# Windowed attention and gated MLP on one core: pairs 0 and 1 loaded and set up ahead of a branch, masks, weights and sinks moved in time, the end spread over four engines

## The chip, the cores and the metric

The kernel runs on one core of one Trainium2 chip. The metric is device time in microseconds of one execution of the whole program, constants, weight conversion, attention and MLP together; lower is better. The core's engines named here are TensorE (PE in the rows, its weight loads PEld), VectorE (DVE), ScalarE (ACT), GpSimd (POOL) and SyncE (SP), which issues nearly all DMAs.

## The reference

Causal attention with a window and a few sink positions, then an MLP whose hidden layer goes through a depthwise convolution of three taps and gates itself:

```python
# q, k, v: (4, 8, 768, 64); n_sink = 4, window = 128 (both are inputs)
rel  = pos[:, None] - pos[None, :]
keep = (pos[None, :] < n_sink) | ((rel >= 0) & (rel < window))
s = np.where(keep, q @ k.T / sqrt(64), -1e9)
a = softmax(s)                                 # sum + 1e-9
x = (a @ v) -> (4, 768, 512)                   # heads side by side
h = maximum(x @ w_in, 0)                       # (4, 768, 1024)
conv = sum over k of conv_w[k] * h shifted by k - 1 along seq
out = (h * sigmoid(conv)) @ w_out              # (4, 768, 512)
```

The activations are float32; w_in, w_out and conv_w reach the kernel as 64-bit floats.

## The kernel before

**Precision.** Each matrix product of two float32 values is made as three products of halves (high x high, low x high, high x low) in TensorE's single-pass 32-bit type. So nearly every tensor passes a split: one engine copies it to the narrow type (xH, gH, wH), another subtracts to get the remainder (xL, gL, wL). Weights come as 64-bit floats; `narrow` puts the two words of each together, with one multiply on ScalarE (L112) and shifts and ors on VectorE, and `split` makes the halves on GpSimd and VectorE.

**Branch.** n_sink and window are loaded into `sc`, copied over all partitions. VectorE makes a flag of them (window between 1 and 128, at most four sinks), every engine reads it, and the program branches to `banded` (which runs here) or to `general`. Up to the branch the first halves of q and k of pair 0 and a half of v are loaded, and an identity matrix is made.

**Attention.** Heads are taken in pairs, 16 pairs, four to a batch. Batch 0 goes in half sequences, all four pairs' first halves and then the second ones; later batches go pair by pair. A job is cut in steps of one row tile of 128. q and k of a half are turned by TensorE (tiles `trq`, `trk`, L319) and copied out and scaled by ScalarE (L250), kinds `X`/`bq` and `kks`/`kk`; then scores on TensorE, mask and row minimum on VectorE (L541, L542), exp on ScalarE (L545), sums and reciprocals on VectorE, scaling on GpSimd. One step later the probabilities are turned (`pT`, L568), and two or three steps later multiplied with v (`pv`). A sink is one of the first four positions; where it lies outside the tile's window its values come from `vsr`, a small tile that holds the v rows of the sinks in split form. It is filled for batch 0 by `sink_load` (L385) and for each later batch by `sink_split` (three loads L396, a copy on ScalarE L397, VectorE L398 to L400, copies by DMA L405). Output of a tile is `px`, split into xH (ScalarE, L351) and xL (VectorE, L352).

**MLP.** `unit` makes one block of 128 hidden rows over 256 positions: 12 matmuls into `ph` (L184: wH·xH, wL·xH, wH·xL, four each), ReLU on ScalarE, the convolution and the gate on ScalarE and VectorE in turn (L191 to L199), the split of the result g (GpSimd, L201 and L202), and 6 matmuls into `po` (L211) which collect over the hidden blocks; after the last block `po` is copied out by ScalarE (L215) and stored (L216). These units are the work that fills TensorE between the steps of the next batch's attention; the last batch's units come after all attention.

**Order.** The code is written in one loop over the steps (D1 = 1, D2 = 2, DL = 3 steps back), with MLP pieces, weights (one per step, list WHEN) and the next job's preparation between the slots. A scheduler then reorders it by simulated times and priorities: steps of attention have a high priority. So code order alone does not say where an instruction stands in its engine's queue. Each engine's queue runs in order. Tiles of the tag "h" are three buffers of TensorE's output memory that q, k, `ph` and other turns share; `pts` is one buffer for turned probabilities of batch 0.

**Masks.** The masks m0, w1 and w2 and the primitives they are made from (`before`, `sk`, `inw`, `prv`, from iotas R and C) stand at the start of `banded`, all on VectorE but for the copy w2 <- w1 (L444, ScalarE) and two narrow copies (L449). GpSimd's memsets there clear `A.zeros` (L454) and `c.vs` (L457); `vsr` is cleared by two DMAs from `A.zeros` (L460).

Of the kernel before, what the change touches and what calls it, by code (L numbers as in the profile page):

```python
# [17 lines left out]
P = 128  # L18
# [43 lines left out]
class Moe:  # L62
# [41 lines left out]
    def narrow(self, raw):  # L104
# [5 lines left out]
        w, low = (self.temp("st", 512, 3)[0:rows, 0:n] for i in range(2))  # L110
        lo, hi, wi, li = raw[:, :, 0], raw[:, :, 1], w.bitcast(I32), low.bitcast(I32)
        nc.scalar.mul(low, f(hi), 2.0 ** -112)  # L112
# [12 lines left out]
    def taps(self, raw):  # L125
        c, nc = self.c, self.c.nc
        w = self.narrow(raw)
        pt = self.ps.tile([P, 512], F32, tag="h", name="cwt", bufs=3)
        c.pin(nc.tensor.transpose(pt[:, 0:3 * self.NFF], w, c.ident[0:3 * self.NFF, 0:3 * self.NFF]))
        nc.scalar.copy(self.cw.rearrange("p k f -> p (k f)"), pt[:, 0:3 * self.NFF])  # L130

    def weights(self):
# [14 lines left out]
        self.raws = []  # L147
        self.done = 0
# [6 lines left out]
    def need(self, n):  # L155

        while self.done < n:
            self.fetch(self.done + 1)
            self.todo[self.done][2](self.raws[self.done])
            self.done += 1  # L160
            self.fetch(self.done + LA)

    def unit(self, n):
# [12 lines left out]
        u = Ctx()  # L176

        def first(lo):
            if lo == 0:
                self.need(max(self.place[f"wi{ff * P // 512}_{self.NCC - 1}"], self.place["taps"]) + 1)  # L180
                u.h = self.ps.tile([P, 512], F32, tag="h", name=f"ph{n}", bufs=3)
            for i in range(lo, lo + 4):
                w, x, cc = prods[i]
                c.pin(nc.tensor.matmul(u.h[:, 0:W], w[:, cc, ff * P:(ff + 1) * P], x[:, cc, t0:t1],  # L184
                                       start=(i == 0), stop=(i == len(prods) - 1)))
# [3 lines left out]
        def gate():  # L189
# [46 lines left out]
class Attn:  # L236
# [20 lines left out]
    def prep(self, g, s, ahead=lambda: None):  # L257
# [20 lines left out]
        def turn_k(half):  # L278
# [24 lines left out]
            if half == 0 and kw > P:  # L303
# [84 lines left out]
def sink_split(c, m, vsr, b):  # L388
# [4 lines left out]
    both = m.mp.tile([P, 512, 2], F32R, tag="nat", name=f"sink{b}", bufs=3).rearrange("p n w -> p (n w)")[0:3 * NS]  # L393
    lo, hi = both[:, 0:512], both[:, 512:1024]
    for part in range(3):
        nc.sync.dma_start(f(lo[NS * part:NS * part + NS]).rearrange("s (h d) -> s h d", d=D), c.v[b].rearrange("h s d -> s h d")[0:NS])  # L396
    nc.scalar.copy(hi, f(lo))  # L397
# [10 lines left out]
def banded(c):  # L408
# [17 lines left out]
    before = cp.tile([P, P], F32, name="before")  # L426
    wprev = cp.tile([P, 1], F32, name="wprev")
    tmps = [m.temp("st", 512, 3) for i in range(2)]
    R, C, inw, sk, tmp, prv = [tmps[i // 3][:, P * (i % 3):P * (i % 3) + P] for i in range(6)]
    c.iotas(R, C)  # L430
    nc.vector.tensor_scalar(before, R, 0.0, None, ALU.is_lt)
    nc.vector.tensor_scalar(sk, C, c.nsv, None, ALU.is_lt)
    nc.vector.tensor_scalar(tmp, R, 0.0, None, ALU.is_ge)
    nc.vector.scalar_tensor_tensor(out=inw, in0=R, scalar=c.wnv, in1=tmp, op0=ALU.is_lt, op1=ALU.mult)
    nc.vector.tensor_scalar(wprev, c.wnv, -float(P), None, ALU.add)
    nc.vector.tensor_scalar(prv, R, wprev, None, ALU.is_lt)
# [7 lines left out]
    nc.scalar.copy(w2, w1)  # L444
    nc.vector.tensor_scalar(w2[:, P:KW], sk[:, 0:NS], -NEG, NEG, ALU.mult, ALU.add)

    def narrow_masks():
        for mk, w in ((m1, w1), (m2, w2)):
            nc.scalar.copy(mk[:, 0:NS], w[:, P:KW])  # L449
# [16 lines left out]
    c.headscale = cp.tile([P, 2], F32, name="headscale")  # L466
    nc.gpsimd.memset(c.headscale, 0.0)
    for j in range(2):
        nc.gpsimd.memset(c.headscale[D * j:D * j + D, j:j + 1], -1.0 / math.sqrt(D))
# [19 lines left out]
    for i, (g, nm, half) in enumerate(queue[0:2]):  # L489
        st[g].raw[nm, half] = c.raw[i]  # L490
    asked = [2]

    free = [RAWB - 2]
# [22 lines left out]
    def scores(g, t):  # L516
# [369 lines left out]
```

## Time and profile before

| | us |
|---|---|
| time, median of 3 runs | 480.58 (479.12 to 481.94) |
| the profiled execution's own time | 479.95 |
| its span on the chip | 478.2 |
| TensorE busy | 447.2 (94%) |
| VectorE busy | 335.9 (70%) |
| ScalarE busy | 321.9 (67%) |
| GpSimd busy | 281.1 (59%) |
| mean granted clock of TensorE (1 is full) | 0.996 |

The span runs from the first to the last instruction of the profiled execution; 1.75 us of its time lie outside. All rows below have their times in us from the start of the span. A row names an engine, a line of the kernel, an operation, and the tiles as out<-in.

### The profile page before, as it was taken

How to read it: one execution, taken by the hardware profiler on the slowest of the kernel's cores; microseconds unless marked ns; L12 is line 12 of the kernel's file. 1: busy time of each engine (PE TensorE's matmuls, PEld its weight loads, DVE VectorE, ACT ScalarE, POOL GpSimd, SP SyncE). 2: the span in 40 equal slices, each digit the busy share in tenths (PEclk: the TensorE clock that was granted, in tenths of full speed). 3: DMA queues.
4: the chain of work that ended last, by engine and by line, in shares of the span. 5: the costliest groups of instructions: out<-in, count | busy, mean ns of one | idle time of the engine just before them, and what ended most of it. 6: DMA issues, size and time to landing. Idle time of an engine off the chain costs nothing.

```text
span 478.2 us, 10559 instructions
## 1 busy us (share of the span) xinstructions
PE 447.2 (94%) x3181; PEld 389.6 (81%) x3181; DVE 335.9 (70%) x1186; ACT 321.9 (67%) x1026; POOL 281.1 (59%) x561
## 2 busy tenths in 40 slices
PE   1888978998999999999999999999999999999993
PEld 1666767897888988898989898988989898988982
DVE  4789989757868668696775858587866653665561
ACT  3898767759868868776775867676866744554541
POOL 3465667633956658667665657567666752445441
PEclk9999999998999999999999999999999999999999
DMA  5778873377695664827273564626361101000001
GB/s 145 202 208 224 238 226 70 77 179 164 162 210 134 160 144 92 206 67 167 69 184 94 122 156 100 157 65 154 75 162 26 45 1 45 0 19 27 31 16 52
DMA packets 105707, 55.91 MB, mean 117 GB/s; under 512 B 83056, under 2 KB 98440, under 8 KB 105640
## 3 DMA queue, kind: packets, MB, share of 16 engines
q1 hardware_dynamic: 105640, 55.13, 46.5%
q8 instruction: 28, 0.46, 0.4%
q14 instruction: 39, 0.32, 0.2%
HBM read 28.17 MB, written 6.29 MB: 72 GB/s over the span
## 4 chain that ended last, share of the span: by engine, by line
PE 68%; DVE 13%; POOL 4%; DMA 4%; ACT 4%; issue 2%; SPq 1%; DVEq 0%; ACTq 0%; POOLq 0%
PE ph L184 24%; PE po L211 23%; PE px L618 7%; PE pts L580 3%; PE sc L344 3%; PE sc L343 3%; PE px L641 2%; PE tq L267 2%; DVE stm L115 1%; DVE t L196 1%; DVE stm L114 1%; DVE t L197 1%; PE tk L293 1%; POOL pe L550 1%; DMA wi_1r<-in_moe_w_in_dram 1%
## 5 line engine op out<-in xcount | busy, mean ns | idle before, releaser
L211 PE MATMUL po<-woH,g 128*128 128x512 f32 x384 | 138.0, 405 | 3.4 <-POOL g L201 3.1
L184 PE MATMUL ph<-xH,wiH 128*128 128x258 f32 (+1 forms) x384 | 111.5, 291 | 2.1 <-DVE xL L352 2.1
L184 PE MATMUL ph<-xH,wiL 128*128 128x258 f32 (+1 forms) x384 | 109.5, 285 | 0.0
L184 PE MATMUL ph<-xL,wiH 128*128 128x258 f32 (+1 forms) x384 | 109.4, 286 | 0.0
L201 POOL TENSOR_SCALAR g<-t 128x256 fp32r<-128x256 f32 x96 | 44.5, 464 | 75.1 <-DVE t L199 56.7
L550 POOL TENSOR_SCALAR pe<-pe,sm 128x132 f32<-128x132 f32 (+1 forms) x144 | 64.1, 457 | 41.7 <-DVE sm L548 27.2
L211 PEld LDWEIGHTS po<-woH,g 128*128 128x128 f32 x384 | 69.4, 189 | 15.3 <-POOL g L201 5.5
L196 DVE SCALAR_TENSOR_TENSOR t<-hb,cw,t 128x256 f32<-128x256 f32 x96 | 53.6, 559 | 37.5 <-ACT t L195 37.1
L202 POOL TENSOR_TENSOR g<-t,g 128x256 fp32r<-128x256 f32 x96 | 74.8, 780 | 5.7
L184 PEld LDWEIGHTS ph<-xH,wiH 128*128 128x128 f32 x384 | 72.8, 190 | 4.9 <-issue 2.5
L211 PE MATMUL po<-woL,g 128*128 128x512 f32 x192 | 76.1, 397 | 0.0
L184 PEld LDWEIGHTS ph<-xH,wiL 128*128 128x128 f32 x384 | 72.9, 190 | 2.2
L184 PEld LDWEIGHTS ph<-xL,wiH 128*128 128x128 f32 x384 | 72.8, 190 | 1.2
L545 ACT ACTIVATE pe<-pe,sm 128x132 f32<-128x132 f32 (+1 forms) x144 | 57.9, 403 | 19.0 <-DVE sm L542 18.1
L198 ACT ACTIVATE t<-t 128x256 f32<-128x256 f32 x96 | 39.9, 417 | 35.2 <-DVE t L197 34.7
L199 DVE SCALAR_TENSOR_TENSOR t<-t,hb 128x256 f32<-128x256 f32 x96 | 46.1, 480 | 16.6 <-ACT t L198 15.4
L195 ACT ACTIVATE t<-hb,cw 128x256 f32<-128x256 f32 x96 | 48.8, 510 | 12.1 <-POOL g L202 9.3
L197 DVE SCALAR_TENSOR_TENSOR t<-hb,cw,t 128x256 f32<-128x256 f32 x96 | 52.0, 541 | 3.9
L191 ACT ACTIVATE hb<-ph 128x258 f32<-128x258 f32 (+1 forms) x96 | 36.8, 384 | 18.9 <-PE ph L184 13.1
L541 DVE COPY_PREDICATED sc<-before,sc 128x128 f32<-128x128 int32 x120 | 32.9, 288 | 18.4 <-PE sc L344 17.8
L618 PE MATMUL px<-pT,vraw 128*64 128x128 f32 (+1 forms) x512 | 42.6, 316 | 2.0 <-ACT pT L568 1.7
L542 DVE CUSTOM_DVE_ANT_0 pe<-sc,m 128x132 f32<-128x132 f32 (+1 forms) x144 | 39.4, 285 | 5.0 <-PE sc L344 4.6
(150 smaller groups left out, 906.9 us busy)
## 6 DMA issues: line engine op xcount, KB each, us to landing
X<-bq SPq DMA_DIRECT2D x96, 96.0 KB
vraw<-in_v_dram SPq DMA_DIRECT2D x16, 384.0 KB
out_dram<-stm SPq DMA_DIRECT2D x24, 256.0 KB
kk<-kk SPq DMA_DIRECT2D x24, 198.0 KB
raw<-in_k_dram SPq DMA_DIRECT2D x24, 192.0 KB
raw<-in_q_dram SPq DMA_DIRECT2D x24, 192.0 KB
kk<-bk SPq DMA_DIRECT2D x48, 96.0 KB
raw<-in_q_dram SPq DMA_DIRECT2D x16, 96.0 KB
```

Source lines behind the costliest of these rows:

```text
L184: c.pin(nc.tensor.matmul(u.h[:, 0:W], w[:, cc, ff * P:(ff + 1) * P], x[:, cc, t0:t1], start=(i == 0), stop=(i == len(prods) - 1)))
L195: nc.scalar.mul(a, prev, cw[:, 0, ff:ff + 1])
L196: nc.vector.scalar_tensor_tensor(out=e, in0=this, scalar=cw[:, 1, ff:ff + 1], in1=a, op0=ALU.mult, op1=ALU.add)
L197: nc.vector.scalar_tensor_tensor(out=a, in0=nxt, scalar=cw[:, 2, ff:ff + 1], in1=e, op0=ALU.mult, op1=ALU.add)
L198: nc.scalar.activation(e, a, AF.Tanh)
L199: nc.vector.scalar_tensor_tensor(out=a, in0=e, scalar=1.0, in1=this, op0=ALU.add, op1=ALU.mult)
L201: nc.gpsimd.tensor_scalar(u.g[:, 0], a, 1.0, 1.0, ALU.mult, ALU.mult)
L202: nc.gpsimd.tensor_tensor(out=u.g[:, 1], in0=a, in1=f(u.g[:, 0]), op=ALU.subtract)
L211: c.pin(nc.tensor.matmul(po[:, 0:c.DM], u.g[:, a, tt * P:(tt + 1) * P], w[:, ff, :], start=(ff == 0 and i == 0), stop=(ff == NFF - 1 and i ...
L545: nc.scalar.activation(pe[:, j, cols], pe[:, j, cols], AF.Exp, bias=sm[:, j:j + 1], scale=-1.0, accum_out=sm[:, 2 + 2 * j:3 + 2 * j])
L550: nc.gpsimd.tensor_scalar(pe[:, j, cols], pe[:, j, cols], sm[:, 8 + j:9 + j], 1.0, ALU.mult, ALU.mult)
L618: ins = nc.tensor.matmul(px[h][D * j:D * j + D, P * at:P * at + n], s.v[:, j, kt, :], pT, start=(h not in open_), stop=False, skip_group_c ...
```

## The change

1. **Loads.** The first halves of q and k of pairs 0 and 1 are loaded ahead of the branch (four slots in place of two); the first half of v goes behind it.
2. **Set-up.** `headscale`, the iotas and the primitives of the masks are made ahead of the branch; three of them carry a dependency (`follow`) on the operation that makes the flag. `follow(c, a, b)` makes a wait for b. The primitives lie in the second v buffer.
3. **Masks.** The copy w2 <- w1 goes to VectorE; GpSimd's two memsets wait for the last mask operation; the two narrow copies wait for the last turned tile; the clearing of `vsr` moves to the middle of batch 0.
4. **Weights.** The first multiply of each `narrow` waits for the exp two steps back (`c.exps[-2]`). The taps are written to another tile and are turned later.
5. **Turns.** In the first halves, every second turn of probabilities uses an "h" tile in place of `pts`; the copy of k's sink columns of the first half moves to the second half's turn.
6. **Sinks.** `sink_split` is cut in two: the loads are issued at the first step of a batch (`sink_fetch`), the split three steps later for every batch (before: at once for batch 1), behind that step's last exp.
7. **End.** The last two units are split on ScalarE and VectorE in place of GpSimd; the unit that has two units behind it (TRAIL) starts its second products only behind the newest first product; the last block of the output is copied by VectorE and ScalarE, half each, and stored by SP's and ScalarE's queues.

The order of ScalarE's queue right behind the branch, before (`trq` and `trk` are the turned q and k, `kks` and `X` their copies, `roomH` rows hold probabilities and masks, `wi_0r` is the first weight):

```order
L250 ACTIVATE kks_155<-trk_187 128x3x128
L328 COPY kks_155<-kks_155 128x6x4
L444 COPY roomH<-roomH 128x260
L449 COPY m_132<-roomH 128x4
L112 ACTIVATE stm_260<-wi_0r 128x512
L449 COPY m_133<-roomH 128x4
L250 ACTIVATE X_184<-trq_180,headscale 128x384 x2
L250 ACTIVATE X_228<-trq_224,headscale 128x384 x2
L545 ACTIVATE roomH,sm_161<-roomH,sm_161 128x128 x2
```

The same place after the change:

```order
L288 ACTIVATE X_182<-trq_178,headscale 128x384 x2
L288 ACTIVATE kks_159<-trk_185 128x3x128
L366 COPY kks_159<-kks_159 128x6x4
L288 ACTIVATE X_224<-trq_220,headscale 128x384 x2
L580 ACTIVATE roomH,sm_163<-roomH,sm_163 128x128
L288 ACTIVATE kks_159<-trk_243 128x3x128
L580 ACTIVATE roomH,sm_163<-roomH,sm_163 128x128
L366 COPY kks_159<-kks_159 128x6x4
L118 ACTIVATE stm_256<-wi_0r 128x512
```

The two copies of q and the first exp have moved ahead of the first weight, and the mask copies are gone.

SP's queue right behind the branch, before:

```order
L101 DMA wi_0r<-in_moe_w_in_dram 128x1024
L363 DMA raw_68<-in_q_dram 128x3x64 x2
L363 DMA raw_68<-in_k_dram 128x3x64
L460 DMA vsr<-roomH 72x768 x2
L385 DMA kks_156<-in_v_dram 4x4x64 x6
L363 DMA raw_68<-in_k_dram 128x3x64
L101 DMA wi_1r<-in_moe_w_in_dram 128x1024
```

After:

```order
L401 DMA vraw_69<-in_v_dram 128x3x64 x2
L106 DMA wi_0r<-in_moe_w_in_dram 128x1024
L401 DMA raw_67<-in_q_dram 128x3x64 x2
L401 DMA raw_67<-in_k_dram 128x3x64 x2
L106 DMA wi_1r<-in_moe_w_in_dram 128x1024
L401 DMA raw_68<-in_q_dram 128x3x64
L423 DMA kks_160<-in_v_dram 4x4x64 x6
L401 DMA raw_68<-in_q_dram 128x3x64
```

The second weight now stands ahead of the six small sink loads, the clearing of `vsr` has left, and v has come in.

ScalarE's queue around the copy of the sinks of batch 1 (`sink`) and the split of batch 0's last output (`xH`), before:

```order
L575 COPY sT_1_1382<-tk_5_1378 96x128
L545 ACTIVATE pe_0_1352,sm_161<-pe_0_1352,sm_161 128x132
L397 CAST sink_1340<-sink_1340 12x512
L545 ACTIVATE pe_0_1352,sm_161<-pe_0_1352,sm_161 128x132
L545 ACTIVATE pe_0_1352,sm_162<-pe_0_1352,sm_162 128x132
L296 CAST kk_1399<-tk_1402 128x3x128
L351 CAST xH_114<-px_1_1450 128x384
```

After:

```order
L389 CAST xH_130<-px_1_1443 128x384
L334 CAST kk_1392<-tk_1395 128x3x128
L334 CAST kk_1392<-tk_1427 128x3x128 x2
L580 ACTIVATE pe_0_1345,sm_163<-pe_0_1345,sm_163 128x132
L619 COPY pT_0_1441<-pts 128x2x128
L247 COPY stm_1623<-po_935 128x512
L580 ACTIVATE pe_0_1345,sm_164<-pe_0_1345,sm_164 128x132
L247 COPY stm_1635<-po_969 128x512
L580 ACTIVATE pe_0_1345,sm_164<-pe_0_1345,sm_164 128x132
L211 ACTIVATE hb_128<-ph_1461 128x260
L288 ACTIVATE bq_1471<-tq_1466 128x384
L440 CAST sink_1341<-sink_1341 12x512
```

The copy of the sinks has gone from four rows ahead of xH to eleven rows behind it.

The core of the diff:

```diff
@@ narrow
-        nc.scalar.mul(low, f(hi), 2.0 ** -112)
+        first = nc.scalar.mul(low, f(hi), 2.0 ** -112)
+        if len(getattr(self.c, "exps", [])) > 1:
+            follow(self.c, first, self.c.exps[-2], "late")
...
@@ unit, gate
+            if left > 1:
+                nc.gpsimd.tensor_scalar(u.g[:, 0], a, 1.0, 1.0, ALU.mult, ALU.mult)
+                nc.gpsimd.tensor_tensor(out=u.g[:, 1], in0=a, in1=f(u.g[:, 0]), op=ALU.subtract)
+            else:
+                nc.scalar.copy(u.g[:, 0], a)
+                nc.vector.tensor_tensor(out=u.g[:, 1], in0=a, in1=f(u.g[:, 0]), op=ALU.subtract)
@@ unit, second
+                if left == TRAIL and tt == 0 and i == 0:
+                    follow(c, ins, self.latest, "last")
...
+                    h = c.DM // 2
+                    nc.vector.tensor_copy(st[:, h:c.DM], po[:, h:c.DM])
+                    nc.scalar.copy(st[:, 0:h], po[:, 0:h])
+                    nc.sync.dma_start(out[:, h:c.DM], st[:, h:c.DM])
+                    nc.scalar.dma_start(out[:, 0:h], st[:, 0:h])
@@ sink_split
-    nc.scalar.copy(hi, f(lo))
+    follow(c, nc.scalar.copy(hi, f(lo)), c.exps[-1], "late")
@@ banded, masks
-    nc.scalar.copy(w2, w1)
-    nc.vector.tensor_scalar(w2[:, P:KW], sk[:, 0:NS], -NEG, NEG, ALU.mult, ALU.add)
+    nc.vector.tensor_copy(w2, w1)
+    masks = nc.vector.tensor_scalar(w2[:, P:KW], sk[:, 0:NS], -NEG, NEG, ALU.mult, ALU.add)
...
-    nc.gpsimd.memset(A.zeros, 0.0)
+    afterwards(nc.gpsimd.memset(A.zeros, 0.0))
...
-    nc.gpsimd.memset(c.vs, 0.0)
+    afterwards(nc.gpsimd.memset(c.vs, 0.0))
@@ banded, transp
+            pt = m.ps.tile([P, 2, 2, P], F32, tag="h", name=f"pt{g}_{t}", bufs=3) if hf == 0 and t % 2 else pts
@@ banded, the loop
             if t == 0 and g and g % NPAIR == 0:
-                after = i + 3 if g > NPAIR else i
+                sinks = sink_fetch(c, m, g // NPAIR)
+                after = i + 3
             if i == after:
-                sink_split(c, m, vsr, g // NPAIR)
+                sink_split(c, vsr, *sinks)
@@ ahead of the branch
-    for i in range(2):
-        load_half(c, 0, "qk"[i], 0, c.raw[i])
-    load_v(c, 0, 0, 0, T // 2)
+    for i in range(RAWB):
+        load_half(c, i // 2, "qk"[i % 2], 0, c.raw[i])
...
+    nc.vector.tensor_scalar(c.before, R, 0.0, None, ALU.is_lt)
+    nc.vector.tensor_scalar(tmp, R, 0.0, None, ALU.is_ge)
+    follow(c, nc.vector.tensor_scalar(c.sk, C, c.nsv, None, ALU.is_lt), flagged, "flag first")
+    follow(c, nc.vector.scalar_tensor_tensor(out=c.inw, in0=R, scalar=c.wnv, in1=tmp, op0=ALU.is_lt, op1=ALU.mult), flagged, "flag first")
+    follow(c, nc.vector.tensor_scalar(wprev, c.wnv, -float(P), None, ALU.add), flagged, "flag first")
+    nc.vector.tensor_scalar(c.prv, R, wprev, None, ALU.is_lt)
```

## Rows read from the trace of the kernel before

**Rows 1.** The page: busy time, share of the span, instructions of each engine.

```profile
PE 447.2 (94%) x3181; PEld 389.6 (81%) x3181; DVE 335.9 (70%) x1186; ACT 321.9 (67%) x1026; POOL 281.1 (59%) x561
```

**Rows 2.** Table by stretch: length; PE, PEld, DVE, ACT, POOL; clock, DMA, GB/s.

```profile
11.10:20.00 8.90, 8.04 (x30) 5.70 (x31) 6.59 (x27) 6.79 (x23) 2.29 (x5) 1.00 0.75 194
...
20.00:30.00 10.00, 8.71 (x67) 6.92 (x66) 7.79 (x36) 10.00 (x36) 5.38 (x12) 1.00 0.85 221
...
30.00:60.00 30.00, 26.21 (x200) 20.71 (x198) 29.16 (x92) 25.53 (x79) 19.52 (x28) 1.00 0.81 225
...
90.00:99.50 9.50, 9.50 (x82) 8.33 (x80) 5.69 (x22) 7.67 (x25) 4.37 (x8) 1.00 0.65 149
...
112.10:115.70 3.60, 3.60 (x19) 3.60 (x19) 1.38 (x9) 3.08 (x11) 1.54 (x4) 0.53 0.55 104
...
135.00:465.00 330.00, 328.87 (x2365) 292.38 (x2362) 224.75 (x803) 218.71 (x708) 200.69 (x408) 1.00 0.40 96
```

**Rows 3.** Waits of TensorE, 6 to 135 us: total us, times, longest.

```profile
PE trq L319 <- DVE wprev L435: 6.9, 1, 6.9
...
PE trq L319 <- DMA raw<-in_q_dram: 3.2, 2, 2.9
...
PE ph L184 <- DVE xL L352: 2.1, 1, 2.1
```

**Rows 4.** Timeline, VectorE and GpSimd, masks: start, duration, operation [idle before <-releaser].

```profile
7.19 0.23 DVE L431 TENSOR_SCALAR before<-stm 128x128 f32<-128x128 f32 x1 [0.38 <-POOL stm L843]
...
8.18 1.47 DVE L432 TENSOR_SCALAR stm<-stm,sc_v 128x128 f32<-128x128 f32 x1
...
7.28 0.83 POOL L454 MEMSET roomH<- 128x792 f32 x1
...
8.06 1.52 POOL L457 MEMSET kks<- 96x1536 f32 x1
```

**Rows 5.** Timeline, the way of the first q and k and of weight 0.

```profile
6.89 0.87 PE L319 MATMUL trq<-ident,raw 128*128 128x128 f32 x3 [6.89 <-DVE wprev L435]
...
8.50 0.49 ACT L250 ACTIVATE kks<-trk 128x384 f32<-128x384 f32 x1 [2.55 <-PE trk L319]
...
10.71 0.66 ACT L112 ACTIVATE stm<-wi_0r 128x512 f32<-128x512 f32 x1
...
11.35 1.99 ACT L250 ACTIVATE X<-trq,headscale 128x384 f32<-128x384 f32 x4
...
13.20 0.28 DVE L542 CUSTOM_DVE_ANT_0 roomH<-sc,m 128x128 f32<-128x128 f32 x1
```

**Rows 6.** Timeline: the sink loads of batch 0 on SP, weight 1 on ScalarE.

```profile
10.70 2.22 SPq L385 DMA_DIRECT2D kks<-in_v_dram  x6
...
18.04 0.67 ACT L112 ACTIVATE stm<-wi_1r 128x512 f32<-128x512 f32 x1 [0.57 <-DMA wi_1r<-in_moe_w_in_dram]
```

**Rows 7.** Timeline: the sinks of batch 1 and the hole behind.

```profile
104.27 0.86 SPq L396 DMA_DIRECT2D sink<-in_v_dram  x2
...
107.45 0.62 ACT L397 CAST sink<-sink 12x512 fp32r<-12x512 f32 x1 [3.07 <-DMA sink<-in_v_dram]
...
108.10 0.68 DVE L398 TENSOR_TENSOR sink<-sink 12x512 fp32r<-12x512 f32 x1 [2.98 <-ACT sink L397]
...
110.88 0.36 PE L184 MATMUL ph<-xH,wiH 128*128 128x260 f32 x1 [2.09 <-DVE xL L352]
```

**Rows 8.** Tile vsr: its users on TensorE (count, mean, from, to), its last copies.

```profile
L641 PE MATMUL px<-sT,vsr x60: 225/275/328, 136.2 to 399.5; 72*128 72x128 f32 x60
...
125.02 1.67 SPq L405 DMA_DIRECT2D vsr<-vsr  x2
```

**Rows 9.** Timeline, the last unit.

```profile
469.98 0.40 POOL L201 TENSOR_SCALAR g<-t 128x256 fp32r<-128x256 f32 x1 [1.94 <-DVE t L199]
...
470.44 0.50 PE L211 MATMUL po<-woH,g 128*128 128x512 f32 x1 [1.19 <-POOL g L201]
...
471.90 1.07 ACT L215 COPY stm<-po 128x512 f32<-128x512 f32 x2 [2.54 <-PE po L211]
```

More of the change, by code (lines that the diff above doesn't have):

```diff
@@ L44, with follow @@
     pass
+def follow(c, ins, other, reason):
+    c.tc.add_manual_dep(ins.ins, other.ins.name, mybir.DependencyInfo(mybir.DependencyClass.Sync, mybir.DependencyReason.DATA),
+                        reason=reason)
 def load_scalars(nc, pool, srcs):
@@ L126, in taps, with turn @@
         c, nc = self.c, self.c.nc
[L127 to L130, printed above, removed]
+        w = self.narrow(raw, self.hb[1][0:3 * self.NFF, 1:P + 1])
+        def turn():
+            pt = self.ps.tile([P, 512], F32, tag="h", name="cwt", bufs=3)
+            ins = c.pin(nc.tensor.transpose(pt[:, 0:3 * self.NFF], w, c.ident[0:3 * self.NFF, 0:3 * self.NFF]))
+            if getattr(c, "exps", []):
+                follow(c, ins, c.exps[-1], "late")
+            nc.scalar.copy(self.cw.rearrange("p k f -> p (k f)"), pt[:, 0:3 * self.NFF])
+        self.owed.append(turn)
     def weights(self):
@@ L161, in need @@
             self.fetch(self.done + LA)
+            if self.owed and self.done == self.place["taps"] + 3:
+                self.owed.pop()()
     def unit(self, n):
@@ L183, in first @@
                 w, x, cc = prods[i]
[L184 to L185 removed]
+                self.latest = nc.tensor.matmul(u.h[:, 0:W], w[:, cc, ff * P:(ff + 1) * P], x[:, cc, t0:t1],
+                                               start=(i == 0), stop=(i == len(prods) - 1))
             if lo + 4 == len(prods):
@@ L302, in turn_k @@
                 nc.sync.dma_start(f(kk[r, 2 + j]), f(s.low[half][r]))
-            if half == 0 and kw > P:
+            if half and kw > P:
                 nc.scalar.copy(s.kk[:, :, :, P:kw], f(s.kk[:, :, 0:1, 0:kw - P]).to_broadcast([P, 4, T, kw - P]))
@@ L425, in banded @@
     m2 = cp.tile([P, KW], F32, name="m2")
[L426 to L436, printed above, removed]
+    before, sk, inw, prv = c.before, c.sk, c.inw, c.prv
     nc.vector.tensor_tensor(out=m0, in0=inw, in1=sk, op=ALU.max)
@@ L465, in banded @@
     A.tiles = 0
[L466 to L469, printed above, removed]
+    c.exps = []
     c.zero = nc.gpsimd.to_reg(0.0)
@@ L488, in banded @@
     queue += [(g, nm, None) for g in range(PLAIN, NG) for nm in "kq"]
-    for i, (g, nm, half) in enumerate(queue[0:2]):
+    for i, (g, nm, half) in enumerate(queue[0:RAWB]):
         st[g].raw[nm, half] = c.raw[i]
-    asked = [2]
-    free = [RAWB - 2]
+    asked = [RAWB]
+    free = [0]
     def ahead():
@@ L838, in attention_gated_mlp @@
     make_identity(nc, c.ident)
+    c.headscale = con.tile([P, 2], F32, name="headscale")
+    nc.gpsimd.memset(c.headscale, 0.0)
+    for j in range(2):
+        nc.gpsimd.memset(c.headscale[D * j:D * j + D, j:j + 1], -1.0 / math.sqrt(D))
     c.identr = con.tile([P, P], F32R, name="identr")
```

70 lines of the change are left out of this document (48 added, 22 removed).

## The prediction

> **What bounds the kernel now.** I read the page first, then the table by stretch, then what TensorE waits for, and last the timeline where it waits. TensorE is busy 447.2 us of the span of 478.2 [rows 1], so about 31 us of idle time are all that a change which removes no matrix work can win, and the question is where they lie. From 135 to 465 us TensorE is busy 328.87 of 330 us while VectorE has 224.75 [rows 2]: there nothing but TensorE counts, and I cost every edit that only touches this stretch at nothing. From 30 to 60 us VectorE is the bound, 29.16 of 30 us; from 20 to 30 us ScalarE is, 10.00 of 10.00, with VectorE at 7.79; from 11.1 to 20 us no engine is full (ScalarE 6.79 and VectorE 6.59 of 8.90), which is a start-up that waits for its own steps [rows 2]. From 90 us on TensorE is full, with one hole: 2.1 us at 108.8 [rows 2, 3], and right behind it, from 112.1 to 115.7 us, a granted clock of 0.53, which is the lower of its two levels (1.2 GHz) for nearly all of that time [rows 2]. The largest waits of TensorE are the 6.9 us up to the branch on the flag and 3.2 us for a load of q just behind it [rows 3].
>
> **The start-up, part by part.** Up to the branch nothing gets shorter: the flag hangs on its two small loads, which stay first in SP's queue, so the 6.9 us stay. SP issues two more loads there (the first halves of q and k of pair 1, and v goes behind the branch); it has until the flag for that, and the loads stand ahead of any that waits.
>
> The masks: four of their operations now stand on VectorE between the flag and its own branch. At 0.23 us each, the row of one that nothing holds up [rows 4], that is 0.9 us, so VectorE enters the body at about 7.5 us and not 6.6. Ten remain behind the branch, 2.2 us, done at about 9.7. Before, the same work lay beside two memsets of GpSimd (0.83 and 1.52 us), and one operation took 1.47 us instead of 0.23 [rows 4]. Now the memsets wait for the masks.
>
> ScalarE's order after the branch is the larger point. Before, the first q, turned by TensorE from 6.89 on (0.87 us), was copied out only at 11.35, since the copy of k, two mask copies and the first weight (10.71, 0.66 us) stood ahead of it; the first score reached VectorE at 13.20 [rows 5]. Now the q copies come first: from 7.76 (6.89 + 0.87), two of 0.5 us (1.99 for four), then k with 0.49 [rows 5], so at 9.25 the first score can run, and VectorE, free at 9.7, takes it at about 9.9. That is 3.3 us earlier. Not all of it is won, because weight 0 had been done before 13.20 and now follows: on ScalarE 0.66 us, on VectorE what lay between 11.37 (10.71 + 0.66) and 13.20, 1.8 us. So ScalarE's lead is 2.6 us and VectorE's 1.5. **I take ScalarE's 2.6 us**, because it is the full engine in the stretch that follows (10.00 of 10.00 from 20 to 30 us) and VectorE has 2.2 us of air there. Behind 30 us VectorE is full and its work is the same, so the lead should be carried, neither grown nor lost. Ends: 1.5 us, if VectorE's idle time stays as it was; 4.7 us, if ScalarE also loses its 2.1 us of idle time between 11.1 and 20 us (8.90 - 6.79) [rows 2].
>
> What speaks against a full lead: the memsets now run from 9.7 to 12.1 (0.83 + 1.52), and the six small sink loads that need the second memset hold SP for 2.22 us [rows 4, 6], to 14.3; half of pair 3's q stands behind them. The second weight's load no longer does: ScalarE began it only at 18.04, waiting for its landing [rows 6]; it is now issued ahead of the sink loads, at about 10.3. The rule that a weight follows the exponential two steps back is a wait of ScalarE on itself; it only keeps the scheduler from drawing weights forward. The second buffer for the transposes, the late turn of the taps and the zeroing of vsr at step 12 have room, and I cost them at nothing; if TensorE had to wait for the shared "h" tiles, the three q and k copies of 0.5 us would be the size of it.
>
> **The sinks of batch 1.** The rows tell the story in order: SP issues two of the three sink loads only at 104.27, behind stores of X; ScalarE sits 3.07 us until they land, starting at 107.45; VectorE sits 2.98 us behind that, starting at 108.10; and the split of the last output of batch 0 (xL), queued behind both, holds TensorE for 2.09 us until 110.88 [rows 7]. In the new order the loads are issued together and ScalarE's step stands 11 rows behind the copy of xH, not four rows ahead of it. TensorE then has, by its order, the same 2.3 us of matrix work between the end of that output and the matmul that needs xL (106.5 to 108.8 in the trace), and ScalarE's copy and VectorE's operations up to xL add to about 2.0 us; so I expect no hole, or a few tenths. Gain 2.1 us. The clock: 19 matmuls took 3.6 us at the lower level; at the pace of 90 to 99.5 us (82 in 9.5, so 0.116 each) they take 2.2 [rows 2]. That is 1.4 us more, 1.8 at most (half of 3.6). **Together 3.5 us**, ends 2.1 and 3.9. The writes of vsr move back in SP's queue, its last copy by two places; that ran at 125.02 for 1.67 us and the first use is at 136.2 [rows 8], so there are 9 us of cover.
>
> **The end.** By the order TensorE's last rows are the same as before, so the wait meant to bring the last unit's first products forward changes nothing there. The last split goes from GpSimd (0.40 us, then 1.19 us of TensorE idle ended [rows 9]) to ScalarE, whose 512 columns take 0.66 [rows 5], so 256 about as long as GpSimd: a gain of 0.1 us from the shorter hand-over. The two last copies took 1.07 us one behind the other on ScalarE [rows 9]; now half of the second runs on VectorE meanwhile, so about 0.8, a gain of 0.3. **Together 0.4 us**, ends -0.2 (the extra operations in ScalarE's and VectorE's queues sit in the last chain) and 1.0. The Trainium skill (DMA: Bandwidth & Descriptors, Anatomy of one DMA) says that a transfer has a fixed cost of about 2 us whatever its size; by that rule two half stores land no sooner than one, and the end would be worth 0.1 to 0.4 us as an estimate; no run here shows it yet.
>
> **Sum.** 2.6 + 3.5 + 0.4 = 6.5 us off the profiled execution's 479.95 (span 478.2), so 473.4. That execution lies 0.6 us under the median of the runs, 480.58, which gives a predicted time of **474.1 us**.
>
> **Rivals.**
> A. The start-up's lead is used up: VectorE has the same work and is full from 30 us, and whatever order it comes in, its end at about 90 us stays. For it: VectorE's own lead is only 1.5 us. Against: it had 4.5 us of idle time between 11.1 and 30. Time 480.58 - 3.9 = 476.7. Chance 0.15.
> B. Another wait takes the place of the sinks: xL comes late all the same, because ScalarE's exponentials and VectorE's scores of the next batch stand ahead of it, and TensorE arrives earlier. For it: my margin is 0.3 us. Time 480.58 - 3.0 = 477.6. Chance 0.11.
> C. It does not do what it says: both A and B, or partial gains under 2.4 us. Time about 480. Chance 0.15.
> D. Slower. The clock falls in the start-up: with its first work done early, TensorE waits in longer single pieces between 12 and 60 us, and one like the 2.09 us ahead of the fall at 112 is enough. At the lower level a matmul of that mix cost 3.6 / 19 = 0.189 us [rows 2]; the 200 of the stretch from 30 to 60 us would then need 37.8 us in place of 30, so 7.8 us are lost and the time is 474.1 + 7.8 = 481.9. It decides from about 25 us at the lower level, where the loss passes 6.5. Against: the wait for q of 2.9 us in one piece [rows 3] was followed by no fall, and the clock came back after 3.6 us of steady work. The Trainium skill (TensorE: Matmul & The Clock Gate, Part 1) says that activity releases the lower level; by that rule a start-up that is busier than before should fall less, and the trace's return at 115.7 agrees. Chance 0.07.
>
> **How the numbers follow.** My forecast has 0.52. A measurement of this kernel tells about 0.5% (2.4 us) from no change. Faster by more than that: forecast, A and B, 0.78; within it: C, 0.15; slower: D, 0.07. The range runs from 470.5 (start-up at 4.7, sinks at 3.9, end at 1.0: 9.6 off would be 471.0, and half a microsecond for the scatter of the runs) to 478.4, which takes in A and B with their bounds and leaves out C's upper part and D.
>
> **What would show it.** Right: VectorE's first score at about 9.9 us; the mask operations at 0.23 us each; the second weight on ScalarE without a wait for its load; no idle time of TensorE over 0.5 us near 105 us and a granted clock of 1.00 from there to the end; TensorE full from about 87 us. Wrong: the first score early but TensorE full only from 90 us (A); a hole of TensorE before the first matmul on batch 0's last xL (B); a granted clock under 1 between 12 and 90 us (D). If the time is under 470 or over 479, a part that I cost at nothing was not nothing.

## The result

The changed kernel takes 474.2 us (median of 5 runs, 472.93 to 475.77) against 480.58 us: a ratio of 0.988, interval 0.9856 to 0.9903. Measured again beside three experiments it took 474.19 us, ratio 0.990 (0.9862 to 0.9934). The forecast was 474.1. The time came out right; the terms of the sum did not all, and part of the agreement is luck: in 63 later runs the kernel before has a median of 479.8 us, 0.8 less than the 480.58 that the forecast started from, so that the change is worth about 5.6 us and not the 6.5 of the sum.

The profiled execution has a span of 471.8 us, 6.4 less than before. The page's busy times of the engines after (before in [rows 1]):

```profile
PE 444.6 (94%) x3181; PEld 388.3 (82%) x3181; DVE 339.0 (72%) x1190; ACT 321.3 (68%) x1027; POOL 281.3 (60%) x557
```

TensorE has the same 3181 matmuls and 2.6 us less busy time, which for the same matmuls means a higher clock, and 3.8 us less idle time. The table by stretch of after, columns as in [rows 2]:

```profile
11.10:20.00 8.90, 8.03 (x37) 5.77 (x36) 6.31 (x30) 7.95 (x28) 2.80 (x5) 1.00 0.77 193
...
30.00:60.00 30.00, 26.85 (x220) 21.91 (x220) 29.14 (x94) 26.73 (x81) 19.16 (x27) 1.00 0.76 214
...
105.00:112.10 7.10, 6.43 (x52) 6.03 (x51) 6.42 (x30) 6.74 (x26) 2.65 (x7) 1.00 1.06 255
112.10:115.70 3.60, 3.60 (x30) 3.34 (x29) 3.52 (x16) 2.61 (x10) 2.99 (x5) 1.00 0.73 179
115.70:135.00 19.30, 17.04 (x119) 14.12 (x119) 13.81 (x64) 14.20 (x52) 15.75 (x35) 1.00 0.61 156
135.00:465.00 330.00, 328.95 (x2354) 293.02 (x2353) 227.96 (x798) 218.11 (x706) 199.67 (x399) 1.00 0.37 95
```

From 112.1 to 115.7 us 30 matmuls run at a clock of 1.00 where 19 ran at 0.53. The sums of the same table over 6.6 to 90 us, first of before, then of after:

```profile
sum 83.40, PE 69.74 PEld 55.45 DVE 75.33 ACT 63.83 POOL 52.71; mean PE 13.95 PEld 11.09 DVE 15.07 ACT 12.77 POOL 10.54
```

```profile
sum 83.40, PE 72.67 PEld 58.04 DVE 76.16 ACT 66.74 POOL 53.19; mean PE 14.53 PEld 11.61 DVE 15.23 ACT 13.35 POOL 10.64
```

TensorE's idle time there falls from 13.7 to 10.7 us. From 90 to 135 us it does not fall: 2.4 us before (all but 0.3 in one hole), 2.9 after. The waits of TensorE in after, 100 to 135 us (total us, times, longest):

```profile
PE sc L381 <- issue: 1.1, 1, 1.1
PE pts L617 <- ACT pT L619: 0.8, 1, 0.8
PE tk L637 <- DVE sk L629: 0.7, 1, 0.7
PE sc L381 <- PE sc L382: 0.4, 1, 0.4
```

One hole of 2.09 us [rows 3] has become four of 0.4 to 1.1 us. The timeline of after, start-up (answers to [rows 4, 5]):

```profile
7.90 1.05 ACT L288 ACTIVATE X<-trq,headscale 128x384 f32<-128x384 f32 x2 [1.93 <-DVE roomH L474]
...
8.82 0.29 DVE L489 TENSOR_TENSOR m<-roomH 128x128 f32<-128x128 f32 x1
...
9.01 0.90 PE L357 MATMUL trq<-ident,raw 128*128 128x128 f32 x3 [0.59 <-ACT X L288]
...
9.92 0.63 PE L378 MATMUL sc<-kks,X 128*128 128x128 f32 x2
...
10.71 0.29 DVE L577 CUSTOM_DVE_ANT_0 roomH<-sc,m 128x128 f32<-128x128 f32 x1 [1.60 <-PE sc L378]
...
11.04 0.40 ACT L580 ACTIVATE roomH<-roomH,sm 128x128 f32<-128x128 f32 x1
...
12.89 0.66 ACT L118 ACTIVATE stm<-wi_0r 128x512 f32<-128x512 f32 x1 [0.48 <-DMA wi_0r<-in_moe_w_in_dram]
```

The masks end at 9.1 us, and VectorE then waits 1.60 us for TensorE, which turns pair 1's q first (9.01, after 0.59 us of waiting for the copies of pair 0's q). So the first score comes at 10.71, 2.5 us earlier than before. The timeline at the sinks and at the end of after (answers to [rows 7, 9]):

```profile
108.33 0.60 ACT L440 CAST sink<-sink 12x512 fp32r<-12x512 f32 x1
...
112.43 0.74 DVE L443 SCALAR_TENSOR_TENSOR sink<-sink,part 12x512 fp32r<-12x512 f32 x1
...
116.84 0.30 PE L381 MATMUL sc<-kk,X 128*128 128x128 f32 x1 [1.05 <-issue]
...
464.20 0.51 PE L239 MATMUL po<-woH,g 128*128 128x512 f32 x1 [0.64 <-ACT g L229]
...
465.90 0.42 DVE L251 COPY stm<-po 128x256 f32<-128x256 f32 x1 [1.30 <-PE po L239]
...
466.36 0.37 ACT L252 COPY stm<-po 128x256 f32<-128x256 f32 x1
466.70 0.65 SPq L253 DMA_DIRECT2D out_dram<-stm  x1
```

### The profile page after: what moved, and what is told of

It reads as the page before. It is cut to its first block, busy times and chain, and to the rows that moved or that the text cites. A ratio compares the mean times of both kernels' runs of the same rounds, so it can differ in the third digit from the quotient of the medians.

```text
span 471.8 us, 10560 instructions
## 1 busy us (share of the span) xinstructions
PE 444.6 (94%) x3181; PEld 388.3 (82%) x3181; DVE 339.0 (72%) x1190; ACT 321.3 (68%) x1027; POOL 281.3 (60%) x557
## 4 chain that ended last, share of the span: by engine, by line
PE 75%; DVE 11%; ACT 4%; POOL 3%; DMA 2%; issue 2%; DVEq 0%; POOLq 0%; ACTq 0%
PE ph L204 26%; PE po L239 25%; PE px L655 7%; PE sc L382 3%; PE sc L381 3%; PE pts L617 3%; PE px L678 2%; DVE stm L122 2%; PE tq L305 1%; PE tk L331 1%; DVE stm L123 1%; DMA kk<-bk 1%; DMA raw<-in_q_dram 1%; DVE roomH L577 1%; DVE roomL L577 1%
## 5 line engine op out<-in xcount | busy, mean ns | idle before, releaser
L586 POOL TENSOR_SCALAR pe<-pe,sm 128x132 f32<-128x132 f32 (+1 forms) x144 | 62.8, 447 | 37.7 <-DVE sm L584 19.2
L216 DVE SCALAR_TENSOR_TENSOR t<-hb,cw,t 128x256 f32<-128x256 f32 x96 | 53.8, 560 | 29.4 <-ACT t L215 28.9
L219 DVE SCALAR_TENSOR_TENSOR t<-t,hb 128x256 f32<-128x256 f32 x96 | 48.3, 504 | 15.1 <-ACT t L218 14.3
L217 DVE SCALAR_TENSOR_TENSOR t<-hb,cw,t 128x256 f32<-128x256 f32 x96 | 54.4, 567 | 4.0 <-POOL pe L586 0.5
L381 PE MATMUL sc<-kk,X 128*128 128x260 f32 (+1 forms) x144 | 42.3, 304 | 1.5 <-issue 1.1
```

Source lines behind the costliest of these rows:

```text
L216: nc.vector.scalar_tensor_tensor(out=e, in0=this, scalar=cw[:, 1, ff:ff + 1], in1=a, op0=ALU.mult, op1=ALU.add)
L217: nc.vector.scalar_tensor_tensor(out=a, in0=nxt, scalar=cw[:, 2, ff:ff + 1], in1=e, op0=ALU.mult, op1=ALU.add)
L219: nc.vector.scalar_tensor_tensor(out=a, in0=e, scalar=1.0, in1=this, op0=ALU.add, op1=ALU.mult)
L381: self.c.pin(self.nc.tensor.matmul(pc, X[:, j, u, :], kk[:, j, lo:hi], start=True, stop=False))
L586: nc.gpsimd.tensor_scalar(pe[:, j, cols], pe[:, j, cols], sm[:, 8 + j:9 + j], 1.0, ALU.mult, ALU.mult)
```

## The experiments

Times are medians; the mean clock is the mean over the runs of TensorE's granted clock in each.

| kernel | us | ratio to before (interval) | mean clock |
|---|---|---|---|
| before (63 runs) | 479.8 | 1 | 0.9963 |
| after; after again (e12) | 474.2; 474.2 | 0.988; 0.990 | 0.9958; 0.9951 |
| e1 before, split later | 479.4 | 0.998 (0.9962 to 1.0001) | 0.9956 |
| e2 after, split at once | 476.2 | 0.991 (0.9883 to 0.9931) | 0.9953 |
| e3 after, sinks early | 476.6 | 0.993 (0.9908 to 0.9959) | 0.9948 |
| e4 after, old end | 475.1 | 0.988 (0.9856 to 0.9908) | 0.9945 |
| e5 after, no wait on exp | 476.3 | 0.993 (0.9909 to 0.9943) | 0.9940 |
| e6 after, two loads | 477.5 | 0.997 (0.9946 to 0.9984) | 0.9943 |
| e7 after, free memsets | 474.7 | 0.990 (0.9882 to 0.992) | 0.9978 |
| e8 after, one turn tile | 476.7 | 0.994 (0.9926 to 0.9962) | 0.9898 |
| e9 masks and set-up only | 478.6 | 0.999 (0.9965 to 1.0018) | 0.9894 |
| e10 after, masks a step early | 476.2 | 0.993 (0.9906 to 0.9956) | 0.9947 |
| e11 start-up only | 476.6 | 0.994 (0.9916 to 0.9964) | 0.9942 |

The clock's column has to be read with the times. In e4's profile it falls twice (table by stretch, columns as above):

```profile
20.00:23.20 3.20, 1.78 (x11) 1.16 (x10) 2.72 (x14) 2.82 (x10) 2.45 (x5) 1.00 0.92 298
23.20:26.60 3.40, 3.40 (x12) 2.19 (x11) 2.30 (x9) 3.02 (x12) 1.86 (x5) 0.50 0.89 211
...
36.90:40.30 3.40, 3.40 (x15) 2.98 (x14) 2.69 (x8) 2.95 (x11) 1.75 (x3) 0.51 0.40 147
```

A stretch of 3.4 us at half the clock costs 1.7 us and lowers the mean over 476 us by 0.0036: 0.001 of mean clock is about 0.5 us, as an estimate. It holds only for stretches in which TensorE works. The mean also takes in the time behind the last matmul, where a low clock costs nothing: in the profile of after, whose mean is 0.997, the clock falls only at 468.8 us, and the last matmul ends at 465.9; in that of e7, whose mean is 0.995, it falls only at 468.8 us too, behind the last matmul at 466.8. So differences of 0.002 between rows of the table say little; those of e8 and e9 are larger than that.

**e1, e2, e3: the sinks.** e1 edits the kernel before, e2 the kernel after:

```diff
-                after = i + 3 if g > NPAIR else i     # e1
+                after = i + 3
...
-                after = i + 3                         # e2
+                after = i + 3 if g > NPAIR else i
...
-            if t == 0 and g and g % NPAIR == 0:       # e3
+            if i == NSTB - 3 or (t == 0 and g > NPAIR and g % NPAIR == 0):
...
```

> The kernel before, with one edit: the split of batch 1's sinks stands three steps later, as it does for the other batches; loads, masks, weights and end are those of before. Theory (place of the split): the 2.09 us hole ahead of the first product on batch 0's last xL goes, the granted clock stays at 1.00 from 105 to 135 us, and the sinks' three VectorE operations (1.9 us) cause smaller holes of 1 to 2.5 us together behind it; so mainly the clock's 1.4 to 1.8 us are won: 480.6 - 1.8 = 478.8 us, ratio 0.996. Rival 1 (as predicted, hole and clock are both won): 480.6 - 3.5 = 477.1, ratio 0.993, with no hole over 0.5 us up to 135. Rival 2 (the late loads made the hole, wherever the split stands): the hole of 2 us and the low clock show up again, 480.6.

> The kernel after, with the split of batch 1's sinks back at the first step of the batch; the loads are still issued together, early. Theory (place of the split): the three VectorE operations stand ahead of xL again, a hole of 1 to 2 us comes back ahead of the first product on xL, and if it is near 2 us the clock falls as well: 474.2 + 1 to 3, so 475 to 477. Rival (the late loads were the cause): ScalarE waits under 0.5 us for the loads, no hole over 0.7 us, clock 1.00, 474.2.

> The kernel after, with batch 1's sinks loaded three steps ahead of the batch's first step and split at that first step; the other batches as in the kernel after. Theory (the four holes behind 111 us, 2.9 us together, come from the sinks' 1.9 us on VectorE): the operations now run at about 95 to 104 us, where TensorE is full and VectorE has 5.4 of 9.5 and 3.1 of 5.5 us, so the holes between 105 and 135 us shrink to 1 us or less and the time is 474.2 - 1.9 = 472.3, ratio 0.983. Rival (they come from the change of batch itself, whose q, k and scores are late on their own): the holes stay at 2.5 to 3 us, 474.2.

e1: the hole is gone and the clock is 1.00 up to 142 us, with holes of 0.2 to 0.6 us behind; the time falls by 1.2 us, with an interval that includes no change. The loads in e1 are not early, so in the profile the later place of the split is enough to close the hole. e2: the waits of TensorE from 90 to 140 us, and the table behind:

```profile
PE pts L617 <- ACT pT L619: 2.0, 1, 2.0
PE sc L381 <- DVE sm L577: 0.5, 1, 0.5
```

```profile
112.10:115.70 3.60, 2.68 (x14) 2.32 (x15) 2.95 (x10) 3.16 (x13) 3.14 (x8) 0.75 0.74 194
```

With early loads but the split at once, a hole of 2.0 us is back, and the time is 2.0 us over after. So the place of the split counts, and not the loads alone; what waits is no longer xL but the turned probabilities. The idle time is not what e2's profile loses: from 90 to 135 us it has 2.5 us of it, after has 2.9. It loses the fall of the clock right behind the hole (113.9 to 117.3 us), 1.7 us. e3 refutes my theory that the sinks' own work on VectorE makes the holes behind 111 us: with that work out of the way they are still there, now with a DMA as releaser (waits of e3, 90 to 140 us):

```profile
PE sc L381 <- DMA kk<-kk: 1.7, 1, 1.7
PE sc L381 <- DMA X<-bq: 0.6, 1, 0.6
```

In e3 they belong to the start of a batch: the first scores wait for copies of k and q that go by DMA. In after the longest of the holes ends at the same kind of matmul, but its row names no releaser ("issue"), so that it has the same cause is likely and not shown. e3 is also 2.4 us slower than after, part of it in the start-up, which the edit doesn't touch: ScalarE waits 1.9 us for the first block of w_out there, which in after it does not (more on that below). The rest is open.

**e4: the end.**

```diff
-            if left > 1:
+            if True:          # the last two splits on GpSimd again
...
-                if left or tt < NT - 1:
+                if True:      # the last output copied and stored whole
```

(and the wait on the newest first product taken out)

> The kernel after, with all of the end undone: the last two units split on GpSimd, the last output copied whole by ScalarE and stored by SP, no wait on the newest first product. Theory: from the last matrix product to the end of the span it takes about 0.3 us longer and TensorE's last wait, 0.64 us in the kernel after, is about 1.2 again: 474.2 + 0.5 = 474.7. Rival 1 (the stores' landing sets the end, so nothing of the copies shows): 474.3. Rival 2 (the wait on the newest first product carries something): over 475.2.

TensorE runs the rows of after in the same order, so the profiles can be laid side by side. e4's last matmul on attention output is 3.3 us later (its two falls of the clock), its span 3.8 us longer, so by this pair the end is worth 0.5 us. Its last copies (timeline of e4):

```profile
467.87 0.49 PE L239 MATMUL po<-woH,g 128*128 128x512 f32 x1 [1.20 <-POOL g L226]
...
469.32 1.07 ACT L247 COPY stm<-po 128x512 f32<-128x512 f32 x2 [2.54 <-PE po L239]
```

The wait of 1.20 us is 0.64 in after. From the last DMA issue to the end of the span it is 4.4 us with two half stores (467.35 to 471.8) and 4.3 before (473.88 to 478.2, its last issues being one row of 1.37 us from 472.51). The Trainium skill (DMA: Bandwidth & Descriptors, Anatomy of one DMA) has a fixed cost of a transfer that doesn't shrink with its size, given there for transfers that GpSimd issues; the stores here, which SyncE and ScalarE issue, agree in that half a store lands no sooner.

The other profiles show that this pair was lucky. Nine of them have the new end and five the old one. The wait is 0.62 to 0.64 us in all nine and 1.19 or 1.20 in all five, but TensorE arrives later with the new end, so from the start of the last first product to the end of that wait only 0.3 us are won (3.96 against 4.27 or 4.28). And from the last issue to the end of the span the two half stores take 4.3 to 5.6 us, 5.1 in the mean, where the whole store takes 4.3 or 4.4. From the last matmul on attention output to the end of the span both ends come to 78.7 us in the mean (78.1 to 79.2 and 78.5 to 78.8). So the shorter wait is real, the halved copies and stores win nothing, and the end as a whole wins nothing that the profiles can show. Why the half stores often land later is not shown; that two queues issue them is one candidate.

**e5 to e8: single parts of the start-up undone.**

```diff
-        if len(getattr(self.c, "exps", [])) > 1:
+        if False:                                   # e5
...
-    for i in range(RAWB):
+    for i in range(2):                              # e6, and v behind pair 1
         load_half(c, i // 2, "qk"[i % 2], 0, c.raw[i])
...
-    afterwards(nc.gpsimd.memset(c.vs, 0.0))
+    nc.gpsimd.memset(c.vs, 0.0)                     # e7, and A.zeros
...
-            pt = m.ps.tile([P, 2, 2, P], F32, tag="h", ...) if hf == 0 and t % 2 else pts
+            pt = pts                                # e8
```

> The kernel after, without the wait of each weight's first multiply on the exp two steps back. By its order weight 0's multiply then stands on ScalarE ahead of the first exp, and its load lands only at 12.9 us. Theory (the start-up's lead is ScalarE's order, so this wait carries a part of it): the first exp moves from 11.04 to about 13.1 us, two us of lead go, 474.2 + 2 = 476.2 us. Rival (as the prediction costed it, nothing): 474.2.

> The kernel after, with only pair 0's first halves of q and k loaded ahead of the branch; pair 1's are the first loads behind it, ahead of v. Theory (the order on ScalarE and the masks carry the lead, not the loads): pair 1's q lands at about 9 to 9.5 us instead of ahead of 9.0, so 0 to 0.7 us are lost: 474.2 to 474.9. Rival (the loads carry the lead): TensorE waits 1.5 us or more for pair 1, 476 or more.

> The kernel after, with GpSimd's two memsets free to run beside the masks. Theory (the masks are not the last thing the first score waits for): one or two mask operations take up to 1.5 us again, the masks end at 10.3 to 10.6 in place of 9.1 us, the first score still starts at about 10.7, and the sink loads go out 1.5 to 2 us earlier: 474.2 plus or minus 0.5. Rival (the masks carry the lead): the first score at 12 us, 475.4 or more.

> The kernel after, with all turned probabilities of batch 0 in the one tile pts again. Theory (VectorE is the bound from 30 to 90 us, so a later turn is hidden; costed at nothing): TensorE waits up to 1 us more for ScalarE's copies of pT between 20 and 60 us, 474.2 plus or minus 0.5. Rival (the second buffer is a part of the start-up's lead): 475 to 477.

e5: weight 0's multiply stands ahead of the first exp, which comes at 12.76 us in place of 11.04 (timeline of ScalarE), and VectorE waits for such multiplies 3.5 us between 12 and 90 us, 0.3 in after:

```profile
12.20 0.66 ACT L118 ACTIVATE stm<-wi_0r 128x512 f32<-128x512 f32 x1 [1.21 <-DMA wi_0r<-in_moe_w_in_dram]
12.76 0.39 ACT L580 ACTIVATE roomH<-roomH,sm 128x128 f32<-128x128 f32 x1
```

```profile
DVE stm L121 <- ACT stm L118: 3.5, 2, 1.9
```

The time is 2.1 us up. In its profile the clock is low from 24.1 to 30.9 us, which alone is 3.4 us. e6: TensorE waits 1.34 us for pair 1's q, and weight 0, whose load stands behind, starts at 14.62 in place of 12.89 (timelines of e6):

```profile
9.72 0.87 PE L357 MATMUL trq<-ident,raw 128*128 128x128 f32 x3 [1.34 <-DMA raw<-in_q_dram]
```

```profile
14.62 0.66 ACT L118 ACTIVATE stm<-wi_0r 128x512 f32<-128x512 f32 x1 [1.56 <-DMA wi_0r<-in_moe_w_in_dram]
```

The time is 3.3 us up, so the rival holds: the loads count. e7: the same mask operation of VectorE in after, and in e7 beside the free memsets (6.82 to 8.91 us on GpSimd), with e7's first score:

```profile
6.60 0.65 DVE L902 TENSOR_SCALAR vraw<-vraw,wprev 128x128 f32<-128x128 f32 x1
```

```profile
6.59 2.67 DVE L902 TENSOR_SCALAR vraw<-vraw,wprev 128x128 f32<-128x128 f32 x1
...
10.69 0.29 DVE L577 CUSTOM_DVE_ANT_0 roomH<-sc,m 128x128 f32<-128x128 f32 x1
```

An operation that takes 0.65 us in after takes 2.67. The Trainium skill (SBUF — State Buffer, SBUF: two separate sides) has a port pair that VectorE and GpSimd lock against each other for a whole instruction, and the one that starts first has it. The trace agrees that VectorE waits: its operation ends at 9.26, 0.35 us behind the memsets. It does not show the second part, since the operation is listed from 6.59 on, ahead of the first memset. The masks still end just in time for the first score, at 10.69, and the time is that of after, within the scatter. e8: TensorE's idle time shows one wait of 2.54 us, and the clock falls as it ends (timeline and table of e8):

```profile
72.24 0.45 PE L610 MATMUL tk<-ident,sk 128*96 128x128 f32 x1 [2.54 <-ACT sk L609]
```

```profile
72.30:75.70 3.40, 3.40 (x16) 3.40 (x17) 2.86 (x9) 3.35 (x10) 2.17 (x4) 0.50 0.03 10
```

All six runs of e8 have a mean clock of 0.994 or less, 0.9898 on average; that is 2.7 us by the estimate above, and the time is 2.5 us up. So by this estimate the clock accounts for all that the second turn tile is worth.

**e9, e11, e10: what is left.** e11 is after with e2's and e4's edits; e9 takes e5's and e8's as well, and e6's two loads, with pair 1's behind the sink loads of batch 0. e10 is a neutral edit:

```diff
-        if i == NSTB - 3:
+        if i == NSTB - 4:
             narrow_masks()
```

> Of the start-up only the set-up and the masks (headscale, mask primitives ahead of the branch, memsets behind the masks, late narrow copies, taps turned late): pair 1's loads stand behind the branch, weights don't wait for an exp, one turn tile, sinks of batch 1 split at once, old end. Theory (the parts of the start-up hold together; each one undone alone gave back 2 to 3 us of it): by its order weight 0's multiply stands on ScalarE ahead of the second exp and waits there for its load until 12.9 us, so little of the lead is left: ratio 0.997 to 1.001, 478 to 481 us. Rival (the prediction's: ScalarE's order at the branch, set by the masks and headscale, carries the lead): ratio 0.994 to 0.995, 476.5 to 478.

> All of the start-up's parts, with the sinks of batch 1 split at once and the old end. Theory (parts add): 474.2 + 2.0 for the sinks (as the split at once cost) + 0.5 for the end = 476.7, or 2.5 us more than the kernel after beside it; against the kernel before 3.9 us or ratio 0.992. Rival (the start-up carries only its 2.6 us): ratio 0.9946.

> The kernel after, with the narrow masks made one step earlier near the end of batch 0: the same work, one step of 4 us earlier, and the scheduler writes some 800 rows of TensorE's queue from there on in another order. Theory 1 (what the experiments lost is what they undid): nothing, 474.2, or the level of the kernel after that runs beside it, within 0.5 us. Theory 2 (any edit reorders the rest and the kernel after has a lucky order): 1 to 2.5 us more than it, with TensorE idle for 1 us more from 102 us on.

> The kernel after itself, beside the other three, as their level: ratio 0.988 against the kernel before, as measured at first (0.9856 to 0.9903).

e11: the start-up alone wins 3.2 us beside the kernel before (479.84 us, measured beside it); with 2.0 for the sinks that makes 5.2, and after beside it is 5.65 faster by the medians, 4.9 by the ratio. So the parts add as far as the scatter lets one see: e11's 3.2 is 1.7 to 4.0 by its interval. e9 wins nothing that can be measured, though its first exp stands at 10.67 us, earlier than in after. Between e9 and e11 the three parts make 1.9 us, and the difference of mean clock, 0.0048, is 2.3 us: by this estimate what e9 lacks is clock. Its profile has 2.0 us less idle time of TensorE up to 90 us than before (11.7 against 13.7), so the lead is there, and falls of the clock take it back. Waits and table of TensorE in it:

```profile
PE tk L610 <- ACT sk L609: 1.8, 1, 1.8
...
PE pts L603 <- ACT cw L142: 1.4, 1, 1.4
```

```profile
39.20:42.60 3.40, 3.27 (x14) 2.22 (x13) 2.75 (x7) 2.88 (x7) 1.59 (x3) 0.50 0.53 174
```

e10 is 2.0 us over after, with an interval that touches after's, while its profile has less idle time of TensorE than after's; its runs spread from 473.3 to 478.4, and the 13 of after from 472.4 to 479.0. Whether a mere change of order costs anything is not settled. It means that 2 us in a single variant (e2, e3, e5) are no proof by themselves; e6, and e9 against after, are clear of it, and e8 has its clock. No experiment is faster than the kernel after.

What spreads the runs of one kernel can be seen in the second profile of after (e12, a run of 478.0 us). ScalarE waits 3.24 us for the first block of w_out, whose multiply stands in its queue ahead of two exps, and TensorE then waits 2.70 us at the turn of the taps (`cwt`), while the clock falls at 35.0 us (timeline of e12):

```profile
33.49 0.66 ACT L118 ACTIVATE stm<-wo0r 128x512 f32<-128x512 f32 x1 [3.24 <-DMA wo0r<-in_moe_w_out_dram]
...
35.68 0.30 PE L139 MATMUL cwt<-ident,hb 24*128 24x24 f32 x1 [2.70 <-DVE hb L123]
```

In the first profile of after the same multiply starts at 31.91 us and the turn of the taps waits 0.14 us; in e3, e4 and e11 ScalarE waits 1.9 to 2.7 us for this load and the turn of the taps 1.4 to 2.1 us. No experiment moves this load or the taps alone.

## Why the prediction was right, and where not

- **What bounds.** Right. From 135 to 465 us TensorE stays full (328.95 of 330), and nearly all was won outside, in 31 us of idle time and a little clock.
- **Start-up, 2.6 us.** 3.2 measured (e11), inside its ends. The masks ended at 9.1 us, sooner than the 9.7 of the forecast. The first score came at 10.71, not 9.9: I left out that TensorE turns pair 1's q ahead of it. TensorE was full from 88.2 us and not from 87 (before: 89.7), but by 90 us it had 2.9 us less idle time, since it had done more of other work by then. The step that failed is the costing at nothing: the exp wait, the loads and the second turn tile were given no price, and undoing each gave 2.1, 3.3 and 2.5 us. Together that is more than the 3.2 of the whole, so these are not terms that add. With all three undone (e9) the first exp still comes early, as the prediction has it, and nothing is won: the order of ScalarE at the branch makes the lead, but without these parts the clock takes it back. The price I named for the tile, three copies of 0.5 us, stood for its waits; they come as one of 2.54, and the clock goes with it. The late turn of the taps, also put at nothing, waits up to 2.70 us in the kernel after itself (e12).
- **The sinks, 3.5 us.** About 2 (e2), or 1.2 when it is the only edit (e1), under the lower end of 2.1, and neither clear of the scatter alone. The hole before xL went, as forecast. What failed is "no hole, or a few tenths": rival B's form came true, in that other waits of 2.9 us in all took the hole's place. Only the clock's part was won in the profile, and it is not there to be won in every run: 33 of the 63 runs of before have a mean clock of 0.997 or more, as high as that of after's profile, which has no such fall.
- **The end, 0.4 us.** The profile of after gave 0.5, but by luck: over all profiles the two ends take the same time. The hand-over, priced at 0.1, gave 0.3; the copies, priced at 0.3, gave nothing, since the two half stores land no sooner and often later.
- **Sum.** 2.6 + 3.5 + 0.4 = 6.5 against 3.2 + 2.0 + 0 = 5.2 by parts. The first comparison gave 6.4, the later one 5.65. So the sinks and the end were too large and the start-up too small, and the rest of the agreement came from a first median of before that was 0.8 us high.
- **Rivals.** A is out: TensorE's lead at 90 us is 2.9 us and is kept. C is out: either comparison is well over its limit of 2.4 us. D was placed rightly: when after ran again, its profile had a clock of 0.51 from 35 to 42 us. It was priced for 30 us at the lower level, 481.9; in that run it held for 7 us and the time was 478.0. It is no rare thing in the kernel after: 4 of its 13 runs have a mean clock of 0.993 or less, against 2 of the 63 of before. In e8 and e9 it decides.

After again, table by stretch:

```profile
30.00:35.00 5.00, 2.98 (x29) 2.18 (x27) 1.98 (x11) 1.76 (x7) 3.05 (x5) 1.00 0.95 290
35.00:42.00 7.00, 6.32 (x32) 5.31 (x34) 5.54 (x21) 5.61 (x18) 2.01 (x3) 0.51 0.56 189
```

## What to carry to other kernels

A hole that is closed at a change of batch shows what was waiting behind it: count the next releasers (here copies by DMA) before you book the whole hole. An edit "with room" in a start-up where several engines are nearly full is not free: ask which single long wait of TensorE it prevents, since such a wait can cost the clock as well (2.54 us and a fall in e8). Look at the clock of several runs before you book a fall that one profile shows. And measure a gain of half a microsecond at the end of a kernel on several profiles: one pair said 0.5 here, and fourteen profiles said nothing.

## What was not expected of the hardware

The clock does not follow the longest hole alone, and one kernel does not always give one course of it. It fell right behind 2.54 us of idle time (e8) and during a wait of 2.70 us (e12), but not behind 2.3 us in one piece at 111 us in e9, nor 2.3 us at 117 in e5, nor 2.1 us at 36 in e11; so D's premise, that one wait like the 2.09 us is enough, does not hold in general. And it fell at 23.2 us in e4, where TensorE had been busy for 1.78 of 3.2 us, but not in e11, where it had been busy for as long in the same stretch (table of e11, against that of e4 above):

```profile
20.00:23.20 3.20, 1.78 (x11) 1.13 (x9) 2.75 (x12) 3.16 (x11) 2.45 (x5) 1.00 0.88 283
23.20:26.60 3.40, 3.32 (x30) 2.63 (x30) 3.01 (x14) 2.73 (x11) 2.39 (x6) 1.00 0.91 218
```

Waits of TensorE from 100 to 135 us and the table behind, both of e9:

```profile
PE ph L204 <- DVE xL L390: 2.3, 1, 2.3
```

```profile
112.00:116.00 4.00, 4.00 (x36) 4.00 (x35) 3.76 (x17) 3.79 (x15) 1.65 (x4) 1.00 0.70 189
```

And the column for the clock reads 1.00 at the start, where matmuls run at half: three transposes take 0.88 us at 13.60 us and 0.49 at 15.44 in after; before, 0.88 at 11.29 and still 0.60 at 16.33. So in these two profiles the busier start also had its full clock earlier. That is a part of the 2.6 us of busy time that I had not counted, about 1 us, since the stretch at 112 us is 1.4 to 1.8 of it.

```profile
13.60 0.88 PE L357 MATMUL trq<-ident,raw 128*128 128x128 f32 x3 [0.38 <-DMA kks<-in_v_dram]
15.44 0.49 PE L357 MATMUL trk<-ident,raw 128*128 128x128 f32 x3
```
